# A retention layer with a multiplicative feed-forward: sharing weight casts between engines and a new written order up to the fourth step

## The chip, the core and the metric

The kernel runs on one core of a Trainium2 chip. The core has five engines that each work through their own queue in order: TensorE (PE; its weight loads are shown apart as PEld), VectorE (DVE), ScalarE (ACT), GpSimd (POOL) and SyncE (SP), whose queue here issues all DMAs. The metric is the device time of one execution in microseconds (us), as the median of several runs.

## What is computed

Two stages follow each other. The first is a recurrence over 768 positions for 4 batches and 8 heads of 64 channels; the second a feed-forward without a nonlinearity, in which two products are multiplied element by element.

```python
gamma = 1.0 - 2.0 ** (-5.0 - np.arange(H))
for t in range(S):
    state = gamma[None, :, None, None] * state + np.einsum('bhd,bhe->bhde', k[:, :, t], v[:, :, t])
    y[:, :, t] = scale * np.einsum('bhd,bhde->bhe', q[:, :, t], state)
x = y.transpose(0, 2, 1, 3).reshape(B * S, H * D)        # 3072 x 512
a = x @ w1                                               # 512 x 1024
b = x @ w2                                               # 512 x 1024
h = a * b @ w3                                           # 1024 x 1024
out = h @ w_out                                          # 1024 x 512
```

All inputs and the output are float32.

## The kernel before

**Work.** W3 and W_out follow each other with nothing between, so the kernel first multiplies them into one matrix of 1024 x 512, kept as eight tiles `W3O[0..7]`. Then it goes through 12 steps of 256 tokens (3 a batch). A step n turns q and k so that channels lie on partitions, computes masked scores, the products of k and v (`kv`) and the running state (`state`), sums both parts of the retention in two PSUM banks (`inter`, `av`), scales them to fp16 (`x_out`), multiplies with W1 and W2 (`a` and `b`), multiplies `a` and `b` (`ht`), and multiplies with `W3O` (`o_unit`, `o_copy`, `o_store`).

**Names of the first part (lines 257 to 298).** `r0..r7` are the row blocks of W3 (128 x 1024), `wo0..wo3` those of W_out, each of 512 KB. `cast_w3(f, engs)` casts block f to fp16 (`w3h`); `turn_w3(f, bank)` transposes it on TensorE in eight pieces into a PSUM bank; `turned_w3(f, eng)` copies that to SBUF (`w3t`); `w3_mm(f, i)` adds the product with W_out's block i, two matmuls of 512 columns; after four such pairs `w3_out(f, eng)` copies the sum to `W3O[f]`. `cast_wo(i, engs)` casts a block of W_out. A string of two engines splits a cast into halves of 512 columns (`split`, line 63): v is VectorE, s ScalarE, g GpSimd. `warm(m)` issues m matmuls on zeros.

**Names of the steps.** `cast("k", n, eng)` and `cast("q", n, eng)` make fp16 values, `cast_v(n, eng)` scales v while casting. `turn` and `turned` transpose k or q on TensorE and copy the result; `dma_turn` does it by a DMA on SP's queue from step 4 on. `mask(n, r, hp)` multiplies scores with a mask on VectorE. `state(n, i)` runs on VectorE, its last index on GpSimd. `fence(n)` is a small ScalarE copy that `inter(n, 1)` stands behind. For the first two steps the products with W1 and W2 are made row block by row block as the weights arrive: `rows(W, n, uh, d)` is four matmuls of 256 columns with weight block d, and `rows_out` evacuates ("a" by ScalarE or VectorE, "b" by VectorE). `cast_w(W, name, d, engs)` casts a weight block; for d 1 and 3 it moves two halves of 64 partitions, one by each engine named, or both by the one. From step 2 on `blk` and `evac` do the same with all weights at hand. `arguments`, `tables`, `late_numbers`, `late_arguments`, `late_tables(p)` and `step_decays` make tables of decays.

**Order.** Nothing is left to a scheduler: the calls at lines 696 to 1375 stand in one written order, each engine takes its own instructions in that order, and what one engine makes for another is passed by semaphores. PSUM has eight banks with the names S0, S1, X0, X1, K, F0, F1 and F2; a bank is written anew when its last reader is done.

**Transfers.** `fetch(name)` issues a load into one of 18 staging buffers; from the nineteenth load on (w10) a buffer is taken over from the load 18 places before, after that was cast. Before, the order is r4, wo0, r1, r2, wo1, r5, wo2, r3, r6, k0, r7, wo3, q0, v0, r0, q1, k1, v1, the eight weight blocks w10, w11, w13, w12, w22, w23, w21, w20, and then k, q and v of steps 2, 3 and 4. Each DMA also waits for the DMA eight places before it in SP's queue.

The lines around the last W3 block before (805 to 811):

```python
    scores(0, ("S1", "X0"), 0)
    scores(0, ("S0", "X1"), 1)
    cast_w3(0, "v")
    w3_mm(3, 3, last=True)
    w3_mm(6, 1)
    mask(0, 0, 1)
    w3_out(3, "s")
```

Of the kernel before, what the change touches and what calls it, by code (L numbers as in the profile page):

```python
# [20 lines left out]
def kernel(  # L21
# [665 lines left out]
    def blk(w, n, u, tag):  # L687
        ab[w, n, u] = two_blocks(W1 if w == "a" else W2, n, u, tag)
# [62 lines left out]
    warm(1, "F2")  # L751
    cast_wo(1, "g")
    w3_mm(1, 0, "S1", first=True)
    warm(2, "F2")
    turned_w3(2, "v")
    w3_mm(1, 1)
    cast_w3(5, "v")
    w3_mm(4, 1)
    w3_mm(2, 1, "X0", first=True)
    w3_mm(2, 0)  # L760
    cast_wo(2, "g")
    late_numbers()
# [12 lines left out]
    turned_w3(3, "v")  # L775
    w3_mm(5, 1)
    turned_w3(6, "v")
    w3_mm(3, 2, "K", first=True)
    w3_mm(3, 1)
    cast("k", 0, "v")  # L780
    w3_mm(6, 0, "F0", first=True)
    cast_w3(7, "g")
    w3_mm(6, 2)
    turn("k", 0, "F1")
    turn_w3(7, "F2")
    cast_wo(3, "v")
# [15 lines left out]
    cast_v(0, "g")  # L802
# [9 lines left out]
    mask(0, 1, 1)  # L812
    kv(0, ("S0", "K"))
    cast("q", 1, "g")
    mask(0, 0, 0)
    w3_mm(7, 1, last=True)
    turn_w3(0, "F2")
    w3_mm(6, 3, last=True)
    state(0, 1)
    w3_out(7, "s")  # L820
    late_arguments()
    inter(0, 0, ("S0", "X1"))
    fence(0)
    turn("q", 1, "S1")
    mask(0, 1, 0)
    w3_out(6, "s")
    cast("k", 1, "g")
    state(0, 2)
    turned_w3(0, "v")
    inter(0, 1)  # L830
    av(0)
    state(0, 3)
    turned("q", 1, "v")
    turn("k", 1, "X0")
    w3_mm(0, 2, "K", first=True)
    cast_v(1, "g")
    turned("k", 1, "s")
    x_out(0, 0)
    w3_mm(0, 0)
    w3_mm(0, 3)  # L840
    x_out(0, 1)
    cast_w(W1, "w1", 0, "s", 0, 512)
    cast_w(W1, "w1", 0, "g", 512, 1024)
    scores(1, ("S0", "S1"), 1)
    scores(1, ("X0", "F0"), 0)
    mask(1, 1, 1)
    w3_mm(0, 1, last=True)
    rows(W1, 0, 0, 0, ("X1", "F1"), first=True)
    mask(1, 1, 0)
    w3_out(0, "s")  # L850
    cast_w(W1, "w1", 1, "vs")
    kv(1, ("S1", "F2"))
    mask(1, 0, 0)
    rows(W1, 0, 1, 0, ("K", "F0"), first=True)
    state(1, 1)
    rows(W1, 0, 0, 1)
    cast_w(W1, "w1", 3, "gs")
    mask(1, 0, 1)
    inter(1, 0, ("S1", "X0"))
    fence(1)  # L860
    state(1, 2)
    rows(W1, 0, 1, 1)
    rows(W1, 0, 0, 3)
    state(1, 3)
    cast_w(W1, "w1", 2, "s")
    inter(1, 1)
    av(1)
    x_out(1, 0)
    rows(W1, 0, 1, 3)
    cast_w(W2, "w2", 2, "g")  # L870
    x_out(1, 1)
    rows(W1, 0, 0, 2, last=True)
    rows(W1, 0, 1, 2, last=True)
    rows_out("a", 0, 0, 1, "s")
    late_tables(4)
# [3 lines left out]
    rows(W1, 1, 0, 0)  # L879
    rows_out("a", 0, 1, 0, "s")  # L880
    rows(W1, 1, 1, 1, ("F0", "F2"), first=True)
    cast_w(W2, "w2", 3, "vv")
    cast_w(W2, "w2", 1, "gs")
    rows(W1, 1, 0, 2)
    rows(W1, 1, 1, 3)
    rows_out("a", 0, 0, 0, "s")
    late_tables(0)
    late_tables(1)
    late_tables(2)
    late_tables(3)  # L890
    rows(W2, 0, 0, 3)
    cast_w(W2, "w2", 0, "v")
    rows(W2, 0, 0, 1)
    rows(W2, 0, 1, 3, ("X1", "K"), first=True)
    rows(W2, 0, 1, 2)
    rows(W2, 0, 1, 1)
    rows(W2, 0, 0, 0, last=True)
    rows(W1, 1, 1, 2)
    rows_out("b", 0, 0, 0)
    rows(W1, 1, 1, 0, last=True)  # L900
    rows(W2, 0, 1, 0, last=True)
    rows_out("b", 0, 0, 1)
# [4 lines left out]
    rows_out("a", 1, 0, 0, "s")
    rows(W2, 1, 0, 2)
    rows_out("b", 0, 1, 0)
    rows(W2, 1, 1, 1, ("S0", "F1"), first=True)  # L910
    rows_out("b", 0, 1, 1)
    cast("k", 2, "g")
# [7 lines left out]
    cast("q", 2, "g")  # L920
    turned("k", 2, "s")
    rows_out("b", 1, 0, 0)
    rows_out("b", 1, 0, 1)
    cast_v(2, "g")
    rows(W2, 1, 1, 0, last=True)
    turn("q", 2, "K")
    o_copy(0, 0)
    turned("q", 2, "s")
    rows_out("b", 1, 1, 1)
    rows_out("b", 1, 1, 0)  # L930
    o_unit(0, 1, ("X0",))
    scores(2, ("S1", "F2"))
    mask(2, 0)
    mask(2, 1)
    o_copy(0, 1)
    kv(2, ("F0", "F1"))
    cast("k", 3, "g")
    o_unit(1, 0, ("K",))
# [467 lines left out]
```

## Time and profile before

| what | value |
|---|---|
| runs without a profile, median (lowest to highest of 3) | 183.72 us (183.13 to 185.54) |
| the profiled execution, whole | 184.67 us |
| its span, first to last instruction | 183.0 us |
| granted TensorE clock, mean | 0.999 |

The profile's page gives each engine's busy time, the chain of work that ended last and groups of instructions; the trace behind it gives each instruction with its start, its length and, in brackets, the idle time of its engine before it with what ended that. Rows in which several instructions are merged carry their number (x8). Busy time of TensorE counts a matmul to its modelled end, so short stalls between overlapping matmuls are partly covered.

### The profile page before, as it was taken

What the parts mean: (1) busy time and instruction counts of PE and PEld (TensorE: products, weight loads), DVE (VectorE), ACT (ScalarE), POOL (GpSimd) and SP (SyncE); (2) the same over time, 40 slices, a digit from 0 to 9 for tenths busy, and PEclk for the clock granted to TensorE, in tenths of its full rate; (3) what the DMA queues carried; (4) which work ended last, traced back from release to release, by engine and by line L of the source; (5) the groups of instructions that cost most, each with busy time, mean ns of one, the idle gap of its engine ahead of it and who ended that gap; (6) DMA issues with size and microseconds to landing.
All of it is one profiled execution on the core that took longest, in us unless ns stands there. A gap on an engine that the chain in (4) does not pass through costs nothing.

```text
span 183.0 us, 6031 instructions
## 1 busy us (share of the span) xinstructions
PE 173.2 (95%) x2626; PEld 124.1 (68%) x2626; DVE 101.7 (56%) x171; ACT 65.0 (36%) x115; POOL 64.7 (35%) x93
## 2 busy tenths in 40 slices
PE   7699979899999999999999999999999999999993
PEld 2355636478865786785876858758778587686872
DVE  2344679973755495648356475383573845644330
ACT  4424414758252521432413323223133142332322
POOL 7236255663656049505245215621254000000000
PEclk9999999999999999999999999999999999999999
DMA  5999999999999999999999999999999442160303
GB/s 208 350 418 367 356 330 387 405 279 240 221 229 250 172 249 216 183 190 182 244 287 174 217 251 201 266 151 226 292 186 221 148 145 88 43 185 8 115 0 115
DMA packets 80025, 40.22 MB, mean 220 GB/s; under 512 B 59392, under 2 KB 73984, under 8 KB 80000
## 3 DMA queue, kind: packets, MB, share of 16 engines
q1 hardware_dynamic: 80000, 39.85, 94.3%
q8 instruction: 20, 0.33, 0.8%
q14 instruction: 5, 0.04, 0.1%
HBM read 29.36 MB, written 6.29 MB: 195 GB/s over the span
## 4 chain that ended last, share of the span: by engine, by line
PE 76%; DMA 11%; DVE 6%; issue 3%; SPq 2%; ACT 0%; DVEq 0%
PE psF L573 36%; PE psF L630 21%; DMA st<-in_k_dram 6%; DMA st<-in_moe_w_dram 4%; PE psF L609 3%; DVE am L408 2%; PE psX L509 2%; PE psX L536 2%; PE psX L630 2%; PE psX L609 2%; SPq L107 2%; PE psS L609 2%; PE psS L394 1%; DVE t L69 1%; PE psK L609 1%
## 5 line engine op out<-in xcount | busy, mean ns | idle before, releaser
L573 PE MATMUL psF<-xt,w 128*128 128x256 f16 x640 | 71.8, 273 | 0.2 <-DVE ht L69 0.2
L573 PEld LDWEIGHTS <-w 128*128 128x128 f16 x640 | 62.5, 98 | 9.5 <-issue 0.3
L69 DVE TENSOR_TENSOR ht<-pa,psF 128x512 f16<-128x512 f32 x43 | 29.6, 687 | 45.3 <-PE psF L573 43.9
L61 ACT COPY pa<-psF 128x512 f32<-128x512 f32 x43 | 25.1, 585 | 42.1 <-PE psF L573 36.9
L630 PE MATMUL psF<-w3o,ht 128*128 128x512 f16 (+2 forms) x184 | 38.5, 361 | 0.3 <-issue 0.3
L630 PEld LDWEIGHTS <-ht 128*128 128x128 f16 x208 | 19.1, 98 | 19.3 <-issue 0.5
L69 POOL TENSOR_TENSOR v<-st,VN 128x1024 f16<-128x1024 f32 x10 | 19.0, 1901 | 24.4 <-DMA st<-in_v_dram 15.9
L648 ACT ACTIVATE osb<-psF 128x512 f32<-128x512 f32 (+2 forms) x22 | 12.3, 558 | 36.6 <-PE psF L630 36.6
L69 POOL TENSOR_TENSOR t<-s,GS 128x256 f16<-128x256 f32 x8 | 5.8, 729 | 31.7 <-DVE s L69 31.7
L554 DVE TENSOR_TENSOR xt<-psX,YN 128x512 f16<-128x512 f32 x19 | 12.8, 724 | 6.6 <-PE psX L536 6.6
L609 PEld LDWEIGHTS <-w 128*128 128x128 f16 x128 | 12.2, 98 | 3.2 <-ACT w L61 1.0
L61 POOL CAST q<-st 128x1024 f16<-128x1024 f32 x11 | 11.4, 1040 | 6.9 <-DMA st<-in_q_dram 6.9
L61 POOL CAST k<-st 128x1024 f16<-128x1024 f32 x11 | 11.4, 1038 | 4.9 <-DMA st<-in_k_dram 4.9
L414 DVE TENSOR_TENSOR am<-psS,keep 128x512 f16<-128x512 f32 x19 | 12.2, 681 | 1.3 <-PE psF L394 1.3
L290 PEld LDWEIGHTS <-w3t 128*128 128x128 f16 x64 | 5.7, 97 | 6.7 <-DVE w3t L61 1.0
L609 PE MATMUL psF<-xt,w 128*128 128x256 f16 x56 | 9.7, 273 | 0.0
L61 DVE CAST w3h<-st 128x1024 f16<-128x1024 f32 x6 | 4.9, 820 | 6.6 <-DMA st<-in_moe_w_dram 6.6
L509 PEld LDWEIGHTS <-t 64*64 64x64 f16 x320 | 5.3, 106 | 4.3 <-issue 3.2
L509 PE MATMUL psX<-qT,t 64*64 64x64 f16 (+1 forms) x296 | 7.8, 199 | 0.2 <-DVE t L69 0.2
L536 PE MATMUL psX<-am,v 64*64 64x64 f16 (+1 forms) x336 | 6.1, 197 | 0.8 <-issue 0.5
L609 PE MATMUL psX<-xt,w 128*128 128x256 f16 x32 | 6.1, 272 | 0.8 <-DVE w L61 0.8
L274 PEld LDWEIGHTS <-w3h 128*128 128x128 f16 x64 | 4.0, 100 | 3.8 <-DVE w3h L61 3.1
(125 smaller groups left out, 184.8 us busy)
## 6 DMA issues: line engine op xcount, KB each, us to landing
st<-in_moe_w_dram SPq DMA_DIRECT2D x16, 512.0 KB, 8.2
st<-in_k_dram SPq DMA_DIRECT2D x20, 256.0 KB, 4.9
st<-in_q_dram SPq DMA_DIRECT2D x10, 512.0 KB, 6.1
st<-in_v_dram SPq DMA_DIRECT2D x20, 256.0 KB, 5.2
out_dram<-osb SPq DMA_DIRECT2D x9, 512.0 KB, 5.7
st<-in_moe_w_out_dram SPq DMA_DIRECT2D x4, 512.0 KB, 7.7
st<-in_k_dram SPq DMA_DIRECT2D x2, 512.0 KB
st<-in_q_dram SPq DMA_DIRECT2D x8, 128.0 KB, 6.2
```

The source lines that it names most:

```text
L61: {"v": nc.vector.tensor_copy, "g": nc.gpsimd.tensor_copy, "s": nc.scalar.copy}[eng](dst, src)
L69: (nc.vector if eng == "v" else nc.gpsimd).tensor_tensor(dst, a, b, op)
L274: nc.tensor.transpose(ps[:, g * 128 : (g + 1) * 128], src[:, c0 : c0 + 255 : 2], ident16[:, :])
L290: nc.tensor.matmul(acc[f][:, :], lhsT=w3t[f][:, g * 128 : (g + 1) * 128], rhs=WO[i][:, r, :], start=(first and r == 0), stop=(last and r = ...
L414: nc.vector.tensor_tensor(t[:, :, :, :].rearrange("p a s i -> p (a s) i"), ps[:, :, :, :].rearrange("p a s i -> p (a s) i"), keep64[:, :]. ...
L509: nc.tensor.matmul(dst, lhsT=TS[n, c][half(r), a, :], rhs=rhs, start=((g, o) not in begun), stop=False, skip_group_check=True,)
L536: nc.tensor.matmul(o, lhsT=v16[n][half(g), t, h * D : (h + 1) * D], rhs=rhs, start=((g, c) not in begun), stop=(n >= EO or t == 1), skip_g ...
L554: nc.vector.tensor_tensor(XT[n][:, :, :].rearrange("p a (s x) -> p (a s) x", s=2)[:, :, g * 64 : (g + 1) * 64].rearrange("p k (i t) -> p k ...
L573: nc.tensor.matmul(ps[:, i, :], lhsT=W[d][:, f * 128 : (f + 1) * 128], rhs=XT[n][:, d, :], start=(i == 0 and d == 0), stop=(i == 1 and d = ...
L609: nc.tensor.matmul(rows_ps[w, n, uh][j // 2][:, j % 2, :], lhsT=W[d][:, f * 128 : (f + 1) * 128], rhs=XT[n][:, d, :], start=(first and j % ...
L630: nc.tensor.matmul(ps[:, :], lhsT=HT[n][:, f, tb * 128 : (tb + 1) * 128], rhs=W3O[f][:, c0:c1], start=(f == 0), stop=(f == 7),)
L648: nc.scalar.activation(o_tile(n, tb)[:, c0:c1], o_ps.pop((n, tb, c0, c1))[:, :], AF.Copy, scale=final_scale)
```

## The change

Only the written order and the engine arguments change; the helpers stay as they are, and all DMAs move the same bytes. The main edits:

- r7 is fetched before k0. k4 is fetched ahead of q3; v3 and v4 are fetched behind q4; q5 is fetched behind those and ahead of the transposing DMAs of step 4; k5 and v5 follow these, then k6 and q6.
- `cast_w3(0)`, the last W3 block, goes from VectorE to halves on GpSimd and ScalarE; on GpSimd it stands behind `cast_v(0)`, on ScalarE between `w3_out(1)` and `w3_out(3)`.
- r2 is cast in halves by GpSimd and ScalarE, r5 by ScalarE and VectorE, r6 by VectorE and GpSimd, r7 by VectorE and ScalarE, wo3 by ScalarE and VectorE.
- The copies `turned_w3(1)`, `(5)` go to VectorE, `turned_w3(3)` to ScalarE. `w3_mm(2, 0)` and `w3_mm(4, 2)` move behind `turn_w3(3)`, `w3_mm(7, 1)` ahead of `kv(0)`.
- `cast("k", 1)` goes to ScalarE, `cast("k", 4)` and `cast("q", 4)` too, `cast("q", 2)` to VectorE.
- W2's blocks: w23 is cast by GpSimd in both halves (before VectorE), w21 by VectorE in both (before GpSimd and ScalarE), w20 by GpSimd (before VectorE).
- The W2 rows of step 0 and W1 rows of step 1 stand in another order, and steps 2 to 4 are interleaved anew up to `inter(3, 1)`.

```diff
+    fetch("r7")
     fetch("k0")
-    fetch("r7")
...
     fetch("k3")
+    fetch("k4")
     fetch("q3")
-    fetch("v3")
-    fetch("k4")
     fetch("q4")
-    fetch("v4")
...
+    warm(1, "F2")
+    step_decays()
+    cast_w3(1, "v")
     w3_mm(4, 0, "S0", first=True)
-    warm(1, "F2")
-    cast_w3(1, "v")
+    cast_w3(2, "gs")
     turn_w3(1, "S1")
     warm(3, "F2")
-    turned_w3(1, "s")
-    cast_w3(2, "v")
+    turned_w3(1, "v")
...
-    cast_w3(5, "v")
+    w3_mm(2, 1, "X0", first=True)
+    cast_wo(2, "g")
+    cast_w3(5, "sv")
+    late_numbers()
     w3_mm(4, 1)
-    w3_mm(2, 1, "X0", first=True)
-    w3_mm(2, 0)
...
-    cast_w3(6, "v")
+    cast_w3(6, "vg")
     w3_mm(5, 0)
     turn_w3(3, "K")
+    fetch("v3")
+    w3_mm(4, 2)
+    w3_mm(2, 0)
+    turned_w3(3, "s")
     turn_w3(6, "F0")
...
-    cast_w3(7, "g")
+    cast_w3(7, "vs")
...
+    cast_v(0, "g")
     w3_mm(4, 3, last=True)
+    cast_w3(0, "gs")
     turned("q", 0, "v")
...
     scores(0, ("S0", "X1"), 1)
-    cast_w3(0, "v")
+    mask(0, 0, 1)
     w3_mm(3, 3, last=True)
     w3_mm(6, 1)
-    mask(0, 0, 1)
+    mask(0, 1, 1)
+    cast("q", 1, "g")
+    w3_mm(7, 1, last=True)
     w3_out(3, "s")
...
+    cast("k", 1, "s")
+    turn("k", 1, "X0")
     turned_w3(0, "v")
...
-    cast_w(W2, "w2", 3, "vv")
-    cast_w(W2, "w2", 1, "gs")
+    cast_w(W2, "w2", 3, "g")
...
+    cast_w(W2, "w2", 1, "v")
...
-    cast_w(W2, "w2", 0, "v")
+    cast_w(W2, "w2", 0, "g")
...
-    cast("q", 2, "g")
+    cast("q", 2, "v")
...
+    cast("k", 4, "s")
     mask(2, 0)
...
+    turn("k", 3, "X0")
     state(2, 1)
     state(2, 2)
+    cast("q", 3, "g")
+    o_copy(1, 0)
+    mask(2, 1)
     state(2, 3)
     inter(2, 0, ("S0", "X1"))
     fence(2)
-    turn("k", 3, "X0")
-    cast("q", 3, "g")
     turned("k", 3, "s")
-    o_copy(1, 0)
+    turn("q", 3, "S1")
     inter(2, 1)
+    cast("q", 4, "s")
```

More of the change, by code (lines that the diff above doesn't have):

```diff
@@ L806 @@
     scores(0, ("S0", "X1"), 1)
-    cast_w3(0, "v")
+    mask(0, 0, 1)
     w3_mm(3, 3, last=True)
     w3_mm(6, 1)
-    mask(0, 0, 1)
+    mask(0, 1, 1)
+    cast("q", 1, "g")
+    w3_mm(7, 1, last=True)
     w3_out(3, "s")
-    mask(0, 1, 1)
     kv(0, ("S0", "K"))
-    cast("q", 1, "g")
+    w3_out(7, "s")
     mask(0, 0, 0)
-    w3_mm(7, 1, last=True)
-    turn_w3(0, "F2")
     w3_mm(6, 3, last=True)
     state(0, 1)
-    w3_out(7, "s")
     late_arguments()
+    w3_out(6, "s")
+    turn_w3(0, "F2")
+    state(0, 2)
     inter(0, 0, ("S0", "X1"))
@@ L825 @@
     mask(0, 1, 0)
[L826 to L829, printed above, removed]
+    state(0, 3)
     inter(0, 1)
     av(0)
-    state(0, 3)
+    cast("k", 1, "s")
+    turn("k", 1, "X0")
+    turned_w3(0, "v")
     turned("q", 1, "v")
-    turn("k", 1, "X0")
+    turned("k", 1, "s")
+    cast_v(1, "g")
     w3_mm(0, 2, "K", first=True)
-    cast_v(1, "g")
-    turned("k", 1, "s")
     x_out(0, 0)
+    cast_w(W1, "w1", 0, "s", 0, 512)
+    x_out(0, 1)
+    cast_w(W1, "w1", 0, "g", 512, 1024)
@@ L839 @@
     w3_mm(0, 0)
     w3_mm(0, 3)
-    x_out(0, 1)
-    cast_w(W1, "w1", 0, "s", 0, 512)
-    cast_w(W1, "w1", 0, "g", 512, 1024)
     scores(1, ("S0", "S1"), 1)
-    scores(1, ("X0", "F0"), 0)
     mask(1, 1, 1)
     w3_mm(0, 1, last=True)
+    scores(1, ("X0", "F0"), 0)
+    mask(1, 1, 0)
     rows(W1, 0, 0, 0, ("X1", "F1"), first=True)
-    mask(1, 1, 0)
+    kv(1, ("S1", "F2"))
     w3_out(0, "s")
     cast_w(W1, "w1", 1, "vs")
-    kv(1, ("S1", "F2"))
+    rows(W1, 0, 1, 0, ("K", "F0"), first=True)
@@ L853 @@
     mask(1, 0, 0)
-    rows(W1, 0, 1, 0, ("K", "F0"), first=True)
     state(1, 1)
+    rows(W1, 0, 1, 1)
+    cast_w(W1, "w1", 3, "gs")
     rows(W1, 0, 0, 1)
-    cast_w(W1, "w1", 3, "gs")
-    mask(1, 0, 1)
[L859 to L863, printed above, removed]
+    inter(1, 0, ("S1", "X0"))
+    cast_w(W2, "w2", 2, "g")
+    fence(1)
+    late_tables(0)
+    state(1, 2)
+    cast_w(W1, "w1", 2, "s")
+    rows(W1, 0, 0, 3)
+    mask(1, 0, 1)
@@ L864 @@
     state(1, 3)
-    cast_w(W1, "w1", 2, "s")
+    late_tables(3)
     inter(1, 1)
     av(1)
-    x_out(1, 0)
[L869 to L875, printed above, removed]
+    x_out(1, 1)
+    rows(W1, 0, 1, 3)
+    rows(W1, 0, 0, 2, last=True)
+    late_tables(2)
+    rows_out("a", 0, 0, 1, "s")
+    rows(W1, 0, 1, 2, last=True)
+    x_out(1, 0)
+    cast_w(W2, "w2", 3, "g")
@@ L893 @@
-    rows(W2, 0, 0, 1)
-    rows(W2, 0, 1, 3, ("X1", "K"), first=True)
+    rows_out("a", 0, 0, 0, "s")
+    rows(W1, 1, 0, 0)
+    rows(W1, 1, 1, 1, ("F0", "F2"), first=True)
+    cast_w(W2, "w2", 1, "v")
+    rows(W1, 1, 1, 2)
+    rows(W1, 1, 1, 3)
+    late_tables(1)
+    rows(W1, 1, 0, 2)
+    rows(W2, 0, 0, 2, ("X0", "F1"), first=True)
+    rows(W2, 0, 0, 1)
+    cast_w(W2, "w2", 0, "g")
+    rows(W2, 0, 0, 3)
+    cast("k", 2, "g")
+    rows(W2, 0, 1, 3, ("X1", "K"), first=True)
+    rows_out("a", 0, 1, 0, "s")
@@ L907 @@
[L907 to L912, printed above, removed]
+    rows(W2, 1, 0, 0, ("X0", "F0"), first=True)
+    late_tables(4)
+    rows(W2, 1, 0, 2)
+    rows_out("a", 1, 0, 0, "s")
+    rows(W2, 1, 1, 1, ("S0", "F1"), first=True)
+    rows_out("a", 1, 1, 1, "v")
     rows(W2, 1, 1, 2)
-    rows(W2, 1, 1, 3)
     rows(W2, 1, 0, 3)
     rows(W2, 1, 0, 1, last=True)
+    rows(W2, 1, 1, 3)
@@ L917 @@
+    cast_v(2, "g")
     rows_out("a", 1, 0, 1, "v")
+    rows_out("b", 1, 0, 1)
+    rows_out("b", 1, 0, 0)
     turn("k", 2, "S1")
+    cast("q", 2, "v")
     o_unit(0, 0, ("X1",))
[L920 removed]
     turned("k", 2, "s")
[L922 to L924 removed]
     rows(W2, 1, 1, 0, last=True)
     turn("q", 2, "K")
[L927 to L932 removed]
@@ L933 @@
-    mask(2, 0)
[L934 to L938, printed above, removed]
+    rows_out("b", 1, 1, 1)
+    o_unit(0, 1, ("X0",))
+    cast("k", 3, "g")
+    turned("q", 2, "v")
+    scores(2, ("S1", "F2"))
+    rows_out("b", 1, 1, 0)
+    kv(2, ("F0", "F1"))
+    o_copy(0, 0)
+    o_copy(0, 1)
+    o_unit(1, 0, ("K",))
+    cast("k", 4, "s")
+    mask(2, 0)
+    turn("k", 3, "X0")
     state(2, 1)
     state(2, 2)
+    cast("q", 3, "g")
+    o_copy(1, 0)
```

110 lines of the change are left out of this document (46 added, 64 removed).

## The prediction

> **What bounds the kernel now.** I read the page first, then the chain of waits, then engine sums by stage, then each engine's timeline up to 70 us.
>
> ```profile
> span 183.0 us, 6031 instructions
> PE 173.2 (95%) x2626; PEld 124.1 (68%) x2626; DVE 101.7 (56%) x171; ACT 65.0 (36%) x115; POOL 64.7 (35%) x93
> ...
> PE 76%; DMA 11%; DVE 6%; issue 3%; SPq 2%; ACT 0%; DVEq 0%
> ```
>
> TensorE is busy for 95% of the span and carries 76% of the chain. The work on it is unchanged by this diff (the same 2626 matmuls), so only the idle time in front of them can be won or lost. The chain says where it lies:
>
> ```profile
> 5.70 11.61 DMA st<-in_k_dram
> 17.32 7.70 DMA st<-in_moe_w_dram
> 25.12 0.06 DVE w3h L61
> ...
> 26.28 1.87 DVE am L408 x3
> ```
>
> Until 25 us the chain is transfers: the last W3 block, r0, lands at 25.0 (17.32 + 7.70). Then VectorE leads: the cast of r0, then masks. The sums by stage (columns: stretch, its length, busy time of PE, PEld, DVE, ACT, POOL, clock, DMA) show how much can be had:
>
> ```profile
> 25.50:30.30 4.80, 3.30 (x67) 1.89 (x66) 4.80 (x9) 1.91 (x4) 2.39 (x3) 1.00 1.10 347
> 33.70:37.20 3.50, 2.37 (x54) 1.52 (x53) 3.44 (x6) 2.57 (x3) 1.14 (x2) 1.00 1.03 410
> 40.30:57.80 17.50, 17.50 (x197) 13.14 (x195) 10.70 (x17) 8.96 (x16) 9.47 (x8) 1.00 1.12 229
> 71.20:165.00 93.80, 93.08 (x1500) 70.08 (x1501) 53.01 (x92) 29.35 (x55) 28.87 (x24) 1.00 1.03 194
> ```
>
> In the first two stretches VectorE is busy all the time and TensorE idles 1.50 and 1.13 us: 2.63 us. From 40.3 to 57.8 TensorE has no idle at all, and from 71.2 to 165 only 0.72 us. So a lead that TensorE has at 40 us reaches the end, unless something in the reordered part eats it. TensorE's own rows (start, length, idle before and who ended it):
>
> ```profile
> 14.07 1.02 PE L290 MATMUL psS<-wo,w3t 128*128 128x512 f16 x4 [0.22 <-POOL wo L61]
> 27.02 0.21 PE L442 MATMUL psS<-v,k 64*64 64x64 f16 x1 [1.12 <-DVE am L408]
> 30.27 0.21 PE L536 MATMUL psX<-am,v 64*64 64x128 f16 x1 [0.38 <-DVE am L408]
> 35.99 0.38 PE L609 MATMUL psX<-xt,w 128*128 128x256 f16 x2 [0.77 <-DVE w L61]
> 36.95 0.21 PE L509 MATMUL psS<-qT,t 64*64 64x128 f16 x1 [0.36 <-DVE t L69]
> 40.30 0.60 PE L609 MATMUL psS<-xt,w 128*128 128x256 f16 x4
> 43.36 0.38 PE L609 MATMUL psX<-xt,w 128*128 128x256 f16 x2
> 58.32 0.21 PE L509 MATMUL psX<-qT,t 64*64 64x64 f16 x1 [0.25 <-DVE t L69]
> ```
>
> Why VectorE is late is in its rows beside GpSimd's:
>
> ```profile
> 19.89 0.69 DVE L61 CAST wo<-st 128x1024 f16<-128x1024 f32 x1 [1.12 <-DMA st<-in_moe_w_out_dram]
> 25.12 1.24 DVE L61 CAST w3h<-st 128x1024 f16<-128x1024 f32 x1 [0.73 <-DMA st<-in_moe_w_dram]
> 28.49 1.13 DVE L61 CAST pos_f<-pos_i 128x256 f32<-128x256 int32 x1
> 34.48 1.36 DVE L61 CAST w<-st 64x1024 f16<-64x1024 f32 x1
> ```
>
> ```profile
> 23.88 1.93 POOL L69 TENSOR_TENSOR v<-st,VS 128x1024 f16<-128x1024 f32 x1 [4.10 <-DMA st<-in_v_dram]
> 26.65 1.04 POOL L61 CAST q<-st 128x1024 f16<-128x1024 f32 x1 [0.83 <-DMA st<-in_q_dram]
> 28.43 1.04 POOL L61 CAST k<-st 128x1024 f16<-128x1024 f32 x1 [0.75 <-DMA st<-in_k_dram]
> 33.19 0.61 POOL L61 CAST w<-st 128x512 f16<-128x512 f32 x1
> 34.26 1.04 POOL L61 CAST w<-st 64x1024 f16<-64x1024 f32 x1 [0.45 <-DMA st<-in_moe_w_dram]
> 43.28 1.04 POOL L61 CAST k<-st 128x1024 f16<-128x1024 f32 x1 [2.50 <-DMA st<-in_k_dram]
> ```
>
> A VectorE cast from SBUF takes 0.69. Started while GpSimd works, it takes 1.24 and ends 0.55 after GpSimd's end (26.36 against 25.81); the third, 1.36, ends 0.54 after (35.84 against 35.30). So VectorE stands until GpSimd's instruction is over. VectorE's masks, which read PSUM, show nothing of this.
>
> **The change part by part.** Every term is a lead of TensorE at a point where the same set of matmuls is behind it in both kernels. Transfers are taken to land as before: the issues before w10 differ only by the exchange of k0 and r7.
>
> *Up to 25 us.* r2, r5, r7 and wo3 are cast in halves on two engines, three copies of turned blocks change sides, step_decays (GpSimd) moves up. ScalarE's half cast costs 0.62, GpSimd's 0.61, and a whole VectorE cast 0.69: nothing is won, and transfers feed these casts. r6 is split between VectorE and GpSimd: in series that is 0.35 (half of 0.69) + 0.61, ready at about 16.5, while its transposes come at 17.1: nothing. k0 now lands behind r7, at 18.7 instead of 17.3; cast by 19.4, turned at 19.75: nothing. One pair of w3_mm fewer stands ahead of 14.07, because w3_mm(2, 0) moved behind it: 0.43 lost there, and scores(0) comes some 0.4 later, at 24.6 to 25.1.
>
> ```profile
> 25.50 0.58 ACT L61 CAST w3o<-psK 128x512 f16<-128x512 f32 x1 [3.02 <-PE psK L290]
> ...
> 32.41 0.62 ACT L61 CAST w<-st 128x512 f16<-128x512 f32 x1
> ```
>
> *25 to 32 us.* r0's cast leaves VectorE. The first mask starts at 25.15 instead of 26.28. kv(0) needs that mask (25.85), the scaled v (25.81) and bank K, whose copy on ScalarE now stands behind ScalarE's half of r0: 25.1 + 0.62 + 0.58 = 26.3. TensorE fills the time with w3_mm(7, 1), which stood behind kv, so kv starts at 26.4 without idle. With one pair more behind it, that is 27.02 + 0.43 - 26.4 = 1.05 lead. GpSimd's half of r0 runs 25.8 to 26.4 and moves the cast of q1 not at all (26.65 waited for its transfer). The cast of k1 goes to ScalarE (28.45 to 29.5), so pos_f at 27.5 finds GpSimd done with q1 (26.4 + 1.04) and costs 0.3 instead of 1.13. The last mask of step 0 ends at 28.8, av(0) starts at 28.85 instead of 30.27: lead 1.4.
>
> *32 to 40 us.* w10 and its successors now arrive only just ahead of their casts. w11's VectorE half runs at 33.0, before GpSimd takes up w13 (34.26, which waited for its transfer), so the 1.36 becomes 0.69 and the idle of 0.77 and 0.36 falls to about 0.4 and 0.25 waiting for ScalarE's half of w11 (33.9) and for w13 (35.2). av(1) comes at 35.85. What then holds is w12, the fourth of the eight weight blocks in SP's queue:
>
> ```profile
> 27.22 0.38 SPq L107 DMA_DIRECT2D st<-in_moe_w_dram  x1
> ```
>
> ```profile
> st<-in_moe_w_dram SPq DMA_DIRECT2D x1, 512.0 KB, 8.2
> ```
>
> It lands at 35.4, and is cast on ScalarE behind a table (late_tables) by 36.85; row units with it take 0.87, the x_out copies end at 37.75, and step 1's rows start at 37.8 instead of 40.30. Seven row units follow in both kernels (0.44 each, (43.36 - 40.30) / 7), the last of them W2's block 2: 40.9 against 43.36. Lead 2.45.
>
> *The W2 casts.* Next wanted is W2's block 1, w21, at 40.9. The last of the eight weight blocks, w20, was issued and landed so:
>
> ```profile
> 30.14 0.33 SPq L107 DMA_DIRECT2D st<-in_moe_w_dram  x1
> ```
>
> ```profile
> st<-in_moe_w_dram SPq DMA_DIRECT2D x1, 512.0 KB, 10.5
> ```
>
> at 40.65; between it and w12 (35.4) the blocks lie 1.31 apart, so w23 lands at 38.0 and w21 at 39.35. The change puts both halves of w23 on GpSimd (about 38.6 to 39.65, and again 1.04) and both halves of w21 on VectorE. Taking turns: VectorE's first half ends 0.55 after 39.65, at 40.2; GpSimd's second 41.25; VectorE's second 41.8. That costs TensorE 0.95. The bounds: no meeting, 39.4 + 2 x 0.69 = 40.8, nothing lost; or VectorE yields to all three queued GpSimd casts (w23 twice, w20, to 41.85) and ends at 43.1, 2.2 lost. I take 0.95: the rows show VectorE going on as soon as one GpSimd instruction ends. Lead 1.5.
>
> The Trainium skill (SBUF — State Buffer, Who interferes with whom) says that a VectorE copy or cast in a 2-port mode and a GpSimd instruction exclude one another, whoever issued first holding the ports for its whole instruction, so a tile shared between these two gains nothing. The VectorE rows agree for one direction (1.24 against 0.69); none shows GpSimd waiting. By the rule the turns above hold; without its second direction GpSimd's second half would end at 40.75 and the cost would sink to at most 0.45.
>
> *40 to 70 us.* q2 is cast on VectorE instead of GpSimd at about 50, k4 and q4 on ScalarE, and evacuations interleave anew. After the last unit of rows(W1, 1, 1, 0) one unit, not two, stands ahead of its bank's reuse, against a ScalarE copy of 0.58: 0 to 0.5 lost over two such places. The state copies before inter(2) stand between the masks instead of behind both, so the 0.25 at 58.32 can go: 0 to 0.4 won with the turned q3 ahead. Together I take -0.1. Where turn("q", 3) moves up, q3 now arrives in sixth place instead of fifth:
>
> ```profile
> 49.77 1.04 POOL L61 CAST k<-st 128x1024 f16<-128x1024 f32 x1 [0.49 <-DMA st<-in_k_dram]
> ...
> 54.04 1.90 POOL L69 TENSOR_TENSOR v<-st,VN 128x1024 f16<-128x1024 f32 x1 [1.41 <-DMA st<-in_v_dram]
> ...
> 58.19 1.04 POOL L61 CAST q<-st 128x1024 f16<-128x1024 f32 x1 [0.86 <-DMA st<-in_q_dram]
> ```
>
> Sixth place lands at 54.0, cast by 55.1, wanted at 57.7: hidden. v3 takes eighth place: 58.2 + 1.9 = 60.1. kv(3) wants it at 63.62 less the lead:
>
> ```profile
> 63.62 0.21 PE L442 MATMUL psX<-v,k 64*64 64x64 f16 x1
> ```
>
> 62.2, so 2.1 to spare. On SP's queue the transposing DMAs of k4 and q4 now stand behind the issue of q5 too; q4's cast on ScalarE ends near 60, where it ended before (58.19 + 1.04 on GpSimd), and scores(4) comes only about 69.
>
> Sum: 2.45 - 0.95 - 0.1 = 1.4 us off the span: 181.6. The profiled execution took 184.67, 1.67 more than its span, so 183.3 for one like it. The runs' median is 183.72, which gives 182.3.
>
> **The rivals.**
> *The W2 casts don't meet* (landings 0.5 us apart from mine would do it; the landings of w23 and w21 are interpolated): the lead of 2.45 stays, 181.3, with the won 0.4 and the idle at 68 us 180.7. Chance 0.2.
> *VectorE is starved*: 2.2 lost instead of 0.95, lead 0.2, 183.5. Against it: no row shows two GpSimd instructions passing a waiting VectorE. 0.12.
> *Nothing is won*: were r0's landing what matters rather than VectorE behind it, w12's landing would rule and the lead of 1.05 would never show; the stages say VectorE is full, so 0.06, 183.7.
> *Slower: v3 too late.* Place eight at 58.2 supposes the loads stay 2.1 apart ((58.19 - 49.77) / 4). kv(3) holds all of TensorE behind it. Landing after 60.3 costs one for one; after 61.7 (3.5 late) the whole is slower than before; three places late (64.5, cast by 66.4) gives 2.8 more than before: 186.5. For it: DMA is full through this stretch, and earlier casts free buffers sooner, so issues bunch. Against it: 2.1 us to spare and unchanged bytes. 0.12.
>
> **How the numbers follow.** The forecast has 0.5 (181.6 to 183.0), the rivals 0.2, 0.12, 0.06 and 0.12. The likeliest is 182.3. The low end takes in the first rival and 0.4 of the runs' spread, 180.3; the high end the starved case, no gain and the milder half of the late v3, 185.0 (its first 1.3 us over before). About 2% of the time, 3.7 us, is what a measurement of this kernel can tell from no change. Faster by that needs 180.05: beyond even the best case, 0.04. Slower by it needs 187.4, v3 over three places late or a wait I have not seen: 0.06. Within: 0.90.
>
> **What would show it.** Right: the first mask near 25.2 and TensorE's idle before kv(0) gone; av(0) near 28.9; step 1's rows near 37.8; VectorE's w21 halves longer than 0.69, each ending 0.55 after a GpSimd cast, and TensorE idle some 0.9 ahead of the W2 rows near 41; the same spacing as before from 71 us. Wrong: rows of step 1 later than 39, TensorE idle before kv(3) with GpSimd waiting for v3's transfer, or new idle from 71 on.

## The result, and the profile after

The changed kernel took 181.44 us (median of 6 runs, 180.42 to 185.68) and the kernel before, run beside it, 183.99 us (6 runs): ratio 0.9843, 95% interval 0.9801 to 0.9884. A second set on another occasion gave 181.84 against 183.79, ratio 0.9897 (0.9852 to 0.9941). Two of the first six executions, 183.56 and 185.68 us, were in a slower state; the ratios use the fast ones alone. So it is faster by 1 to 2%: clear of noise, and inside the 2% that the prediction took as the line. The profiled execution took 181.46 us, 1.76 more than its span; before it was 184.67.

The page of the changed kernel, the same parts as shown of before (span, busy time by engine, chain by engine):

```profile
span 179.7 us, 6033 instructions
PE 172.8 (96%) x2626; PEld 123.7 (69%) x2626; DVE 100.1 (56%) x172; ACT 67.9 (38%) x120; POOL 64.5 (36%) x93
...
PE 75%; DMA 12%; SPq 4%; ACT 3%; POOL 2%; DVE 1%; issue 1%; POOLq 0%
```

VectorE's share of the chain fell from 6% to 1%, and "issue" from 3% to 1%. The span is 3.3 us shorter, while TensorE's busy time is only 0.4 less: idle time went away. The sums by stage (columns as before: stretch, its length, busy PE, PEld, DVE, ACT, POOL, clock, DMA, GB/s):

```profile
24.00:28.50 4.50, 4.50 (x92) 2.44 (x90) 3.92 (x10) 2.31 (x5) 3.53 (x3) 1.00 1.06 295
28.50:33.00 4.50, 4.50 (x94) 2.70 (x93) 3.75 (x8) 3.21 (x5) 3.22 (x3) 1.00 1.02 391
33.00:37.80 4.80, 4.65 (x107) 3.14 (x106) 4.02 (x8) 4.12 (x8) 2.02 (x2) 1.00 1.03 411
55.00:68.00 13.00, 12.84 (x242) 9.70 (x243) 8.06 (x16) 5.84 (x10) 5.99 (x5) 1.00 1.20 202
68.00:165.00 97.00, 97.00 (x1700) 73.41 (x1691) 54.96 (x95) 30.48 (x59) 30.28 (x25) 1.00 0.97 197
```

From 24 to 33 us TensorE has no idle time left and VectorE has some (3.92 of 4.50). From 33.0 to 37.8 TensorE idles 0.15, from 55 to 68 it idles 0.16. TensorE's rows at the points where the prediction counted its lead (start, length, instruction, idle before it; the last is the first block of step 3's products with all of W1 and W2 at hand):

```profile
26.77 0.21 PE L442 MATMUL psS<-v,k 64*64 64x64 f16 x1
29.18 0.21 PE L536 MATMUL psX<-am,v 64*64 64x128 f16 x1
38.50 1.03 PE L609 MATMUL psS<-xt,w 128*128 128x256 f16 x8
41.69 0.39 PE L609 MATMUL psX<-xt,w 128*128 128x256 f16 x2
61.63 0.19 PE L442 MATMUL psX<-v,k 64*64 64x64 f16 x1 [0.16 <-POOL v L69]
72.47 0.27 PE L573 MATMUL psF<-xt,w 128*128 128x256 f16 x1
```

The products with all weights at hand come in 64 matmuls a step from step 2 on, and the row at 72.47 is the 65th of them, so it belongs to step 3. The texts on record below call the same row "step 5's blocks", and the row at 134.46, which is step 8's, "step 10"; times and differences are the same under either name.

Two more rows of the kernel before, needed from here on: the same first block of step 3, and a stall late in its trace.

```profile
74.59 0.27 PE L573 MATMUL psF<-xt,w 128*128 128x256 f16 x1
118.94 0.23 PE L536 MATMUL psX<-am,v 64*64 64x64 f16 x5 [0.47 <-issue]
```

Against the rows of before, kv(0) came 0.25 sooner with one more pair of w3_mm behind it, av(0) 1.09, step 1's rows 1.80 (40.30 to 38.50), the W2 rows 1.67 (43.36 to 41.69), step 3's blocks 2.12. Five steps later the same line has 134.46 before and 131.15 after, a lead of 3.31. The last 1.19 is not something that the changed kernel does: TensorE is never idle in it from 68 to 165 us, and the kernel before stalled there on "issue", as in the row at 118.94.

VectorE and GpSimd around the places that the diff touches:

```profile
25.49 0.69 DVE L408 TENSOR_TENSOR am<-psS,keep 128x512 f16<-128x512 f32 x1 [0.58 <-PE psX L385]
27.92 0.28 DVE L61 CAST pos_f<-pos_i 128x256 f32<-128x256 int32 x1
33.68 0.69 DVE L61 CAST w<-st 64x1024 f16<-64x1024 f32 x1
39.28 0.91 DVE L61 CAST w<-st 64x1024 f16<-64x1024 f32 x1 [0.83 <-DMA st<-in_moe_w_dram]
40.20 1.43 DVE L61 CAST w<-st 64x1024 f16<-64x1024 f32 x1
```

```profile
39.69 1.41 POOL L61 CAST w<-st 64x1024 f16<-64x1024 f32 x1
59.67 3.86 POOL L69 TENSOR_TENSOR v<-st,VN 128x1024 f16<-128x1024 f32 x2 [4.20 <-DMA st<-in_v_dram]
```

VectorE now waits for TensorE before its first mask, pos_f costs 0.28 instead of 1.13 and w11's half 0.69 instead of 1.36. At 39 us two casts of w21 meet three casts of weights that GpSimd began at 38.61: 0.91 and 1.43 instead of 0.69, and 1.41 for the second half of w23 instead of 1.04.

### The profile page after: what moved, and what is told of

It is laid out like the page before. It is cut to its first block, busy times and chain, and to the rows that moved or that the text cites. A ratio compares the mean times of both kernels' runs of the same rounds, so it can differ in the third digit from the quotient of the medians.

```text
span 179.7 us, 6033 instructions
## 1 busy us (share of the span) xinstructions
PE 172.8 (96%) x2626; PEld 123.7 (69%) x2626; DVE 100.1 (56%) x172; ACT 67.9 (38%) x120; POOL 64.5 (36%) x93
## 4 chain that ended last, share of the span: by engine, by line
PE 75%; DMA 12%; SPq 4%; ACT 3%; POOL 2%; DVE 1%; issue 1%; POOLq 0%
PE psF L573 38%; PE psF L630 20%; DMA st<-in_moe_w_out_dram 5%; DMA st<-in_v_dram 4%; DMA st<-in_k_dram 3%; SPq L99 2%; PE psX L509 2%; PE psK L290 2%; PE psF L290 2%; PE psX L290 2%; PE psX L536 2%; PE psS L394 1%; ACT pa L61 1%; POOL v L69 1%; PE psS L290 1%; SPq L107 1%
## 5 line engine op out<-in xcount | busy, mean ns | idle before, releaser
L61 POOL CAST q<-st 128x1024 f16<-128x1024 f32 x9 | 9.4, 1042 | 7.4 <-DMA st<-in_q_dram 4.4
L61 POOL CAST k<-st 128x1024 f16<-128x1024 f32 x9 | 9.6, 1064 | 6.7 <-DMA st<-in_k_dram 3.7
L61 POOL CAST w<-st 64x1024 f16<-64x1024 f32 (+2 forms) x6 | 6.5, 1084 | 3.1 <-DMA st<-in_moe_w_dram 2.9
L69 POOL TENSOR_TENSOR v<-st,VS 128x1024 f16<-128x1024 f32 x2 | 3.9, 1933 | 8.7 <-DMA st<-in_v_dram 8.7
L61 ACT CAST w3h<-st 128x512 f16<-128x512 f32 (+1 forms) x5 | 3.5, 704 | 9.1 <-DMA st<-in_moe_w_dram 9.1
```

Of the source, the lines that this page charges most:

```text
L61: {"v": nc.vector.tensor_copy, "g": nc.gpsimd.tensor_copy, "s": nc.scalar.copy}[eng](dst, src)
L69: (nc.vector if eng == "v" else nc.gpsimd).tensor_tensor(dst, a, b, op)
```

## The experiments

Each kernel was run beside the kernel before; a lead in them is counted against the profile of before (rows of step 1 at 40.30, step 3's blocks at 74.59).

**The kernel before again.** No edit.

> The kernel before, unchanged, profiled once more. In its first profile TensorE stood 0.42 us at 96.8 (among o_unit matmuls) and 0.65 us at 118.3 (among av matmuls) with nothing that it waited for; together with a smaller one 1.2 us, and the changed kernel's profile has none of them. Theory 1 (they are strays of one execution): other places or none this time, blocks of step 10 some 1.2 us earlier than 134.46 and span about 181.8. Theory 2 (they belong to the kernel): both again at the same instructions, span about 183.0. Step 1's row products (first at 40.30) and step 5's blocks (first at 74.59) within 0.2 of the first profile in either case.

Measured: 184.45 against 184.49, ratio 1.0004 (0.9966 to 1.0041). Rows at 40.32, step 3's blocks at 74.61: within 0.02 of the first profile. The stall came again, at the very same matmul (number 1757 in order of start, counted from 0, near the end of step 7's av), and the one that ended at 97.41 did not:

```profile
119.10 0.23 PE L536 MATMUL psX<-am,v 64*64 64x64 f16 x5 [1.03 <-issue]
```

So the two profiles agree to 0.02 up to step 3 and not behind it. That agreement is closer than it is in general: two kernels below have the order of before up to step 1's rows, and there the rows came at 40.63 and 40.80, since r0 landed later (its cast began at 25.77 and 26.00, against 25.12). A lead counted against 40.30 can be off by up to 0.5.

**r0 alone.** In the kernel before:

```diff
-    cast_w3(0, "v")
+    cast_w3(0, "gs")
```

> The kernel before with one edit: the last W3 block is cast by GpSimd and ScalarE in halves instead of by VectorE. Theory 1 (VectorE's 1.24 us cast holds the masks, and what it gives is kept): first mask near 25.2 instead of 26.28, kv(0) at 26.3 to 26.6 instead of 27.02, av(0) about 0.6 to 1.0 earlier, step 1's rows 0.5 to 1.0 earlier than 40.30, and 0.5 to 1.0 us off the time. Rival (the weights' arrival sets step 1, so r0 alone is worth nothing): av(0) earlier but step 1's rows at 40.2 to 40.4 and the time within 0.3 us of before. Rival 2 (the halves hurt: ScalarE's copy of bank K and GpSimd's q1 stand behind them): kv(0) at 27.0 or later, time 0 to 0.5 longer.

Measured: 182.51 against 184.49, ratio 0.9894 (0.9848 to 0.9939). Rows from its timelines, of VectorE (first mask, pos_f, half of w11) and of TensorE:

```profile
26.02 0.69 DVE L408 TENSOR_TENSOR am<-psS,keep 128x512 f16<-128x512 f32 x1 [0.65 <-PE psX L385]
28.24 0.29 DVE L61 CAST pos_f<-pos_i 128x256 f32<-128x256 int32 x1
34.00 0.69 DVE L61 CAST w<-st 64x1024 f16<-64x1024 f32 x1
...
30.37 0.62 PE L358 MATMUL psX<-ident,k 128*128 128x128 f16 x8
39.16 0.27 PE L609 MATMUL psS<-xt,w 128*128 128x256 f16 x1
73.44 0.27 PE L573 MATMUL psF<-xt,w 128*128 128x256 f16 x1
```

One word of the diff gives a lead of 1.14 us at step 1's rows (40.30 to 39.16), and 1.15 are left at step 3. Little of it comes from the masks directly: the first starts only 0.26 sooner, not the 1.1 that was expected, since it waits for the scores, and kv(0) 0.21 sooner (26.81). There TensorE waits until 27.12 for bank K, whose copy on ScalarE had itself waited 0.23 for TensorE's product in it, and not for ScalarE's half of r0. The lead comes from what stands behind on VectorE. pos_f takes 0.29 instead of 1.13, because it now runs before GpSimd's cast of k1 (28.88), and TensorE reaches the transposes of k1 at 30.37 instead of 30.84. VectorE's half of w11 takes 0.69 instead of 1.36, because it runs before GpSimd's cast of w13 (34.48), and the row units with w11 come at 35.14 instead of 35.99. So the cast of r0 made VectorE late enough to meet GpSimd twice more.

**r0 back on VectorE,** in the changed kernel, where the kernel before had it:

```diff
-    cast_w3(0, "gs")
...
     scores(0, ("S0", "X1"), 1)
+    cast_w3(0, "v")
     mask(0, 0, 1)
```

> The changed kernel with one edit undone: the last W3 block is cast whole by VectorE, ahead of the masks of step 0, as before. Theory 1: the cast meets GpSimd's scaling of v again and takes about 1.2, first mask near 26.6 instead of 25.49, av(0) about 1.0 later than 28.93, step 1's rows 0.5 to 1.0 later than 38.50, 0.5 to 1.0 us longer than the changed kernel. Rival (weights' arrival sets step 1): step 1's rows within 0.2 of 38.50, time within 0.3 of the changed kernel.

Measured: 181.99 against 184.49, ratio 0.9887 (0.9832 to 0.9941).

```profile
25.05 1.21 DVE L61 CAST w3h<-st 128x1024 f16<-128x1024 f32 x1 [0.17 <-DMA st<-in_moe_w_dram]
...
38.97 0.27 PE L609 MATMUL psS<-xt,w 128*128 128x256 f16 x1
72.76 0.27 PE L573 MATMUL psF<-xt,w 128*128 128x256 f16 x1
```

The cast costs 1.21, as it did before, yet the rows come only 0.47 later than in the changed kernel, just under the 0.5 to 1.0 that was expected, and step 3's blocks 0.29. The first blocks arrived alike in the two profiles (transposes of the second W3 block at 8.76 and 8.78), so the 0.47 isn't a matter of arrival. The edit gives 1.14 by itself, and taking it out of the changed kernel costs 0.47, so the edits overlap. What the others do in its place was not tried one by one; the profile has pos_f at 0.28 here as well, since the cast of k1 is not on GpSimd.

**Early half, late half.** One kernel has the changed order and loads up to step 1's last rows and the old ones behind; the other the reverse (both cut at):

```
turn("k", 2, "S1")
```

> The changed kernel's order up to the last row products of step 1, then the order, casts and loads of before from the turning of k2 on. Theory 1 (most of the gain is made before 40 us and kept): step 1's rows at 38.5, step 5's blocks at 72.8 to 73.2 (before 74.59, changed 72.47), time 1.5 to 1.8 us under before. Rival (the new order of steps 2 to 4 is what keeps the lead): the lead shrinks to under 0.8 by step 5, blocks of step 5 later than 73.8.

> The kernel before up to step 1's last row products, then the changed kernel's order, casts and loads from the turning of k2 on. By the profiles so far the late order takes away the idle of 0.45 (before inter of step 2) and 0.32 (among the blocks of step 2) and adds a wait for v3 of up to 0.32. Theory 1: from step 1's rows (40.30) to step 5's blocks 33.8 to 34.0 us instead of 34.29, so blocks of step 5 at 74.1 to 74.3; v3 is wanted later here than in the changed kernel, so its wait is 0 and the gain may reach 0.7. In the time 0.4 to 0.7 us, plus up to 1.2 if the stall of TensorE at 118 us goes too. Rival (late order is worth nothing alone): 34.2 or more, blocks of step 5 at 74.5 or later.

Measured: early 182.1 against 184.49, ratio 0.9896 (0.9839 to 0.9953); late 183.05 against 184.14, ratio 0.995 (0.9919 to 0.9981). Of the early half:

```profile
37.80 0.27 PE L609 MATMUL psS<-xt,w 128*128 128x256 f16 x1
72.28 0.27 PE L573 MATMUL psF<-xt,w 128*128 128x256 f16 x1
```

Of the late half:

```profile
40.63 0.27 PE L609 MATMUL psS<-xt,w 128*128 128x256 f16 x1
74.21 0.27 PE L573 MATMUL psF<-xt,w 128*128 128x256 f16 x1
```

The early half has a lead of 2.50 at the rows and 2.31 at step 3's blocks, so it keeps it, and the rival in which only the new order of steps 2 to 4 keeps the lead fails. Taken from the rows of step 1 to step 3's blocks, so that the landing of the first blocks drops out, the old order takes 34.29 (before) and 34.48 (early half), the new 33.58 (late half) and 33.97 (changed kernel). The late order is worth 0.71 by itself, and with the early half in front of it 0.3 to 0.5 by this profile. The 0.32 that TensorE waits for v3 there is in the difference: a lead brings TensorE sooner to transfers that don't come sooner. A second profile of the changed kernel, without that wait, took 33.78. The profile of the late half stalled like before at step 7 (0.62 us idle ahead of 118.41), which is in that execution's time, 184.21, and not in the 0.71.

**v3 fetched sooner.** In the changed kernel's first list of loads:

```diff
     fetch("q3")
+    fetch("v3")
     fetch("q4")
+    fetch("v4")
+    fetch("q5")
...
-    fetch("v3")
...
-    fetch("v4")
...
-    fetch("q5")
```

> The changed kernel with v3 fetched ahead of q4, one place sooner, and v4 and q5 in the row of first loads too. Theory 1 (eighth place makes v3 late: kv(3) waited 0.32 us for its cast): v3's cast ends 2 us sooner, no idle before kv(3), step 5's blocks 0.3 sooner counted from step 1's rows (33.6 to 33.7 us instead of 33.97), 0.3 us off the time. Rival (another wait stands right behind it, VectorE's state copies or q4's later transposing): 33.9 or more, time unchanged within 0.2.

Measured: 181.82 against 184.14, ratio 0.9865 (0.9818 to 0.9913). v3's multiplication on GpSimd, then TensorE:

```profile
56.51 1.90 POOL L69 TENSOR_TENSOR v<-st,VN 128x1024 f16<-128x1024 f32 x1 [1.06 <-PE psX L358]
...
41.55 0.28 PE L609 MATMUL psX<-xt,w 128*128 128x256 f16 x1
61.26 0.21 PE L442 MATMUL psX<-v,k 64*64 64x64 f16 x1
72.11 0.27 PE L573 MATMUL psF<-xt,w 128*128 128x256 f16 x1
```

kv(3) no longer waits. But in this execution the rows began 0.32 sooner (38.18), and the wait for w21 grew from 0.13 to 0.31: the 28 matmuls up to the W2 row took 3.37, against 3.06 before. From there to step 3's blocks it took 30.56 against the changed kernel's 30.78. From the rows it took 33.93, so the 33.6 to 33.7 that was expected did not come, and a gain in the time isn't shown either: 181.82 against 181.44 and 181.84 of the changed kernel.

**The pair ahead again.** In the changed kernel `w3_mm(2, 0)` was put back ahead, behind `turn_w3(5, "X1")`.

> The changed kernel with one pair, w3_mm(2, 0), moved back ahead of the first product with W_out's block 2, into TensorE's idle of 0.61 at 14.0. Theory 1 (TensorE has no idle from 14.3 to 34, so a pair done ahead is a lead kept): scores of step 0 about 0.4 sooner, kv(0) 0.2 to 0.4 sooner unless bank K's copy holds it, step 1's rows 0.2 to 0.4 sooner than 38.50, time 0.2 to 0.4 lower. Rival (the weights' arrival, w12 at 35.4, holds step 1): step 1's rows within 0.15 of 38.50 counted from the same arrival, time unchanged.

Measured: 181.49 against 184.14, ratio 0.9857 (0.9814 to 0.99). Of this kernel the cast of k0, ScalarE's half of wo3 and a product with wo3, and then the same product in the changed kernel:

```profile
18.95 0.69 DVE L61 CAST k<-st 128x1024 f16<-128x1024 f32 x1 [0.68 <-DMA st<-in_k_dram]
...
20.15 0.62 ACT L61 CAST wo<-st 128x512 f16<-128x512 f32 x1 [1.92 <-DMA st<-in_moe_w_out_dram]
...
20.82 0.59 PE L290 MATMUL psX<-wo,w3t 128*128 128x512 f16 x2
```

```profile
20.81 0.59 PE L290 MATMUL psX<-wo,w3t 128*128 128x512 f16 x2
```

Both reach it at 20.8, and step 1's rows at 38.50. The lead is 0.38 at the transposes of r6 (16.93 against 17.31). It is 0.21 at those of k0 (19.70 against 19.91), which wait for the cast of k0, a block that only lands at 18.9. The rest goes at 20.82, where the product waits for ScalarE's half of wo3 (20.15 + 0.62), which only lands at 20.1. The place of this pair costs nothing.

**One warm matmul more,** in the kernel before, to move the stall:

```diff
-    warm(8)
+    warm(9)
```

> The kernel before with nine instead of eight warming matmuls on zeros at the start, which end before the first W3 block is cast (4.66 against 4.95), so the order of work is untouched and TensorE's queue is two instructions longer from the start on. In both profiles of before TensorE stood at the same matmul of step 7's av (0.65 and 1.22 us, ending at 118.9 and 119.1) with nothing that it waited for, and a 16 KB instruction transfer had ended 1.3 us earlier each time. Theory (TensorE waits there for its instructions): the stall, if it comes, is two instructions earlier in the work, at matmul 1755 of the old count. Rival (it belongs to that matmul or to a time): it stays at the same matmul of av, or at 118.9 to 119.1. If there is none, it is a stray that the alignment or the run decides. Time within 0.3 of before, or 0.8 to 1.2 less if the stall goes.

Measured: 184.4 against 184.14, ratio 1.0042 (1.0001 to 1.0083). Its profile has no stall (span 182.4 against 183.0, with the rows 0.5 later, since r0's cast began 0.88 later), but the median did not fall. So it does not show that the stall weighs on most executions of before, nor that it doesn't.

**w21 shared between VectorE and ScalarE,** in the changed kernel:

```diff
-    cast_w(W2, "w2", 1, "v")
+    cast_w(W2, "w2", 1, "sv")
```

> The changed kernel with one edit: W2's block w21 is cast by ScalarE and VectorE, a half each, instead of both halves by VectorE, so only one VectorE cast can meet GpSimd's two casts of w23. Theory 1 (taking turns with GpSimd makes w21 late, at 41.5 to 41.8, and TensorE waits 0.13 to 0.31 for it): w21 ready by 40.5, 28 row units after step 1's first take 3.06 instead of 3.19, 0.1 to 0.3 us off the time. Rival (ScalarE's evacuations, now behind its half of w21, hold bank K or X1): the same stretch 3.2 or longer, time unchanged or up to 0.5 longer.

Measured: 182.13 against 183.79, ratio 0.9898 (0.9852 to 0.9944).

```profile
38.91 0.91 DVE L61 CAST w<-st 64x1024 f16<-64x1024 f32 x1 [0.52 <-DMA st<-in_moe_w_dram]
...
38.44 0.27 PE L609 MATMUL psS<-xt,w 128*128 128x256 f16 x1
41.53 0.27 PE L609 MATMUL psX<-xt,w 128*128 128x256 f16 x1
116.46 0.25 PE L536 MATMUL psX<-am,v 64*64 64x64 f16 x5 [0.91 <-issue]
```

VectorE has one half left and the 28 matmuls take 3.09, with the wait for w21 gone (3.19 in the changed kernel). It is worth 0.1 in the profile, and the time shows no gain (the changed kernel beside it took 181.84). Here the stall, 1.10 us of TensorE's time, is in a kernel that has the changed order: it isn't a property of the old one.

**The three together, and the changed kernel beside it.** v3 sooner, the pair ahead and w21 shared in one kernel; and the changed kernel without an edit.

> The changed kernel with three edits together: w21 shared by ScalarE and VectorE, v3 fetched one place sooner, and the pair w3_mm(2, 0) ahead of W_out's block 2. Theory 1 (the two waits, for w21 and for v3, are what the changed kernel still loses in this part): from step 1's rows to step 5's blocks 33.5 us instead of 33.97, 0.4 to 0.5 us faster than the changed kernel in the profile; the pair adds nothing, as it did alone. Rival (each wait taken away uncovers the next): 33.8 or more and the time within 0.2 of the changed kernel.

> The changed kernel, unchanged, profiled once more beside the two others on one chip. Theory 1: from step 1's rows to step 5's blocks 33.9 to 34.0 us, w21's second half over 1.3 us, kv(3) idle 0.2 to 0.4, no stall of TensorE at step 7's av, span 179.3 to 180.1. If the stall near 118 us is a stray that any kernel may have, it can show here and then adds 0.6 to 1.2.

Measured: together 181.24 (180.8 to 181.96), ratio 0.9869 (0.9829 to 0.991); changed kernel 181.84 (181.01 to 182.55), ratio 0.9897 (0.9852 to 0.9941). The intervals overlap, so a gain of the three over the changed kernel isn't shown. Of the three together:

```profile
38.24 0.27 PE L609 MATMUL psS<-xt,w 128*128 128x256 f16 x1
71.89 0.27 PE L573 MATMUL psF<-xt,w 128*128 128x256 f16 x1
79.61 0.29 PE L394 MATMUL psS<-qT,kT 64*64 64x64 f16 x12 [0.19 <-DMA qT<-q]
```

Of the changed kernel again:

```profile
38.09 0.38 PE L609 MATMUL psS<-xt,w 128*128 128x256 f16 x2
61.02 0.21 PE L442 MATMUL psX<-v,k 64*64 64x64 f16 x1
71.87 0.27 PE L573 MATMUL psF<-xt,w 128*128 128x256 f16 x1
```

The waits for w21 and v3 are gone in the first, and a new one, for q5's transposing DMA ahead of scores(5), stands at 79.6. In the second kv(3) found v3 ready, without any edit: both kernels reach step 3's blocks at the same time, 33.65 and 33.78 after step 1's rows. Neither expectation held as it stood (33.5, and 33.9 to 34.0). The wait for v3 is a chance of an execution, of some 0.3 us; w21's second half took 1.43 in both profiles of the changed kernel.

## Why the prediction was right

The forecast was 182.3, faster but within 2%, and so it came: 181.44 and 181.84 lie in its range of 180.3 to 185.0, the first just under the 181.6 to 183.0 that had half of the chance. The sum behind it was right by less than it seems, and in part by luck: two of its errors cancel, and a gain of 0.45 was put at -0.1. By the profiles the lead at step 3's blocks is 1.80 - 0.13 + 0.45 = 2.12, where the prediction had 2.45 - 0.95 - 0.1 = 1.4.

- **VectorE behind r0: right.** Its first mask starts at 25.49 (25.15 predicted), kv(0) at 26.77 without idle (26.4), av(0) at 29.18 (28.85), each some 0.35 late. The mask waits for TensorE's scores, so r0's landing no longer holds it. r0 alone gives 1.14 and keeps it, which refutes the rival in which w12's landing rules; most of it is gained at pos_f and w11, the two places that the prediction priced behind the first mask. That VectorE stands until a GpSimd instruction is over, and that pos_f and w11 escape it, came out as counted (0.28 and 0.69).
- **"0.43 lost" up to 25 us: wrong.** The pair ahead again gains nothing at 20.82 or 38.50: the landings of k0 and then of wo3 take it back. The prediction had counted k0's landing behind r7 as free by itself and did not see that it helps to make the pair free too.
- **Step 1's rows at 37.8: mis-sized,** 38.50. Two things end just ahead of them. The second x_out copy ended at 38.45, where 37.75 was predicted. The cast of w12 ended at 37.46 instead of 36.85, and with the two row units behind it (0.87) it leads to nearly the same point. By the written order both stand behind TensorE's row units with w11. These began at 34.52, where the prediction has 33.9, since VectorE's half of w11 ran at 33.68 and not at 33.0, behind a mask that waited for scores of step 1:

```profile
34.52 0.38 PE L609 MATMUL psK<-xt,w 128*128 128x256 f16 x2
36.43 1.03 ACT L61 CAST w<-st 128x1024 f16<-128x1024 f32 x1
37.77 0.68 DVE L552 TENSOR_TENSOR xt<-psS,YS 128x512 f16<-128x512 f32 x1
```

The early half, with the same order and the first blocks 0.96 sooner, had the rows at 37.80, so the size of this term is also a matter of arrival. In the seven row units behind it the prediction misread one place: the last of them uses W2's block 2 in the changed kernel and block 3 before. Their number is the same, and so is the lead.

- **W2 casts, 0.95: the mechanism right, the price wrong.** VectorE and GpSimd took turns one instruction at a time, and w21 was ready at 41.63 (40.20 + 1.43), where 41.8 was predicted. The Trainium skill (SBUF — State Buffer, Who interferes with whom) says that whoever issued first holds the shared ports for its whole instruction and the other blocks fully; here both directions are seen, 0.91 and 1.43 for VectorE's 0.69, and 1.41 for GpSimd's 1.04. But the price of a late block depends on when it is wanted, and TensorE, itself 0.7 late, came at 41.56: 0.13 lost. The two errors cancel, which is luck: 2.45 - 0.95 = 1.5, against 1.80 - 0.13 = 1.67. v3 sooner confirms it from the other side, since with rows 0.32 earlier the same casts cost 0.31. Neither rival on these casts held: they met, and VectorE was not passed over.
- **40 to 70 us, -0.1: wrong by sign.** Two idles of before, 0.45 at 58.3 and 0.32 at 68.1, are gone, and one of 0.32 came at kv(3) (each counted between the starts of the matmuls around it, less the usual spacing; the idle that the rows show is less): 0.45 won. The 0.45 at 58.3 is the place of the state copies that was offered as "0 to 0.4 won", and the 0 to 0.5 to be lost at two ScalarE copies did not come: TensorE has no idle from 42 to 55 us. The late half alone (34.29 to 33.58) shows it.
- **v3 too late, the slower rival:** it came closer than its chance of 0.12 says. v3 was to land at 58.2 with 2.1 us to spare; GpSimd began it at 59.67, waiting for the transfer, so 1.5 of it was used by the transfer, and the rest by TensorE's greater lead. In the second profile of the changed kernel the wait was not there.
- **"The same spacing as before from 71 us": wrong for the profile of before.** 1.07 us of the 3.31 are two stalls on "issue" in it (0.42 ahead of 97.41, 0.65 ahead of 118.94), which the changed kernel doesn't have in its two profiles. How much of the medians' difference they make stays open: the intervals of the two sets give 2.13 to 3.66 and 1.08 to 2.72 us, and the 2.12 without any stall lies in the second and at the edge of the first.

## What to carry to other kernels

Where one engine is full just ahead of the bound engine, moving a single instruction off it can give most of what a large reordering gives (1.14 of 1.80 us here), the more so where the instructions behind it then no longer meet another engine's; the edits around it then overlap rather than add. Price a block that comes late by when it is wanted, not by when it is ready: rows 0.32 sooner raised the price of the same late block from 0.13 to 0.31. A wait that is removed can uncover another close behind (the pair ahead, the three together). Before the late part of a trace is put down to a change, take a second profile of the unchanged kernel, and compare at points ahead of its stray stalls.

## What the runs showed of the hardware

**A stall at the same matmul, unrelated to any wait.** In 4 of 13 profiles (the kernel before twice, the late half, w21 shared) TensorE stood 0.65 to 1.22 us at matmul 1757 (in the late half at the one before it), put down to "issue". In each the thirteenth of the 16 KB transfers of the page's instruction queue (20 packets, 0.33 MB) ended shortly before:

| profile | transfer ends | that matmul starts | difference |
|---|---|---|---|
| before | 117.66 | 118.94 | 1.28 |
| before again | 117.75 | 119.10 | 1.35 |
| late half | 116.78 | 118.41 | 1.63 |
| w21 shared | 115.07 | 116.46 | 1.39 |

In the nine profiles without the stall that matmul came 1.44 to 2.05 after the end of that transfer. That the matmul waits for its instructions fits this, though the two sets overlap (1.63 with, 1.44 without); it was not tried by itself. The shorter stall of before fits it as well: it ended at 97.41, 384 matmuls ahead of the other one and 1.46 after the end of the tenth transfer (95.95), three transfers ahead of the thirteenth. The Trainium skill (Runtime: NRT & Kernel Launch, Instruction fetch mechanics) says that instructions come in 16 KB blocks, fetched while earlier ones run, at a cost that is mostly hidden; the traces agree on the size, and where this reading holds, up to 1.22 us were not hidden. Why the transfer is late in some executions is open.

**The first blocks land up to 1.2 us apart between executions.** The transposes of r1, the second W3 block, began between 7.82 and 9.02 us. In the kernel before a later block can be hidden: its two profiles are 0.45 apart at one W3 product (14.94 and 15.39) and 0.04 at kv(0) (27.02 and 27.06), because VectorE waited for r0 in between. Where r0 itself landed later (late half, one warm matmul more), kv(0) came at 27.67 and 27.86. In the changed kernel, dense from 14.3 us on, the arrival carries through: five profiles with its order up to step 1's rows have them between 37.80 and 38.50, but all 29.7 to 30.0 us after the transposes of r1. So single profiles of variants can't be told apart below about 0.7 us unless they are compared from the same arrival.
